# A linear-attention and feed-forward kernel: its written list of steps made anew, and the last block's rows stored in two halves

## The chip, the cores and the metric

The kernel runs on one core of a Trainium2 chip. A core has TensorE (PE in the profile; its weight loads are shown apart as PEld), VectorE (DVE), ScalarE (ACT), GpSimd (POOL) and SyncE (SP). SP only issues DMA transfers, on its own queue (q1 in the profile); GpSimd issues others on a second one (q0). The metric is the device time of one execution, in microseconds.

## The reference

The first part is a gated linear attention over 4 batches, 8 heads, 768 positions and a head width of 48. The second is a feed-forward layer over the 3072 rows that it gives.

```python
f = 1.0 / (1.0 + np.exp(-f_logit))                       # all inputs (4, 8, 768, 48)
for t in range(S):
    state = f[:, :, t, :, None] * state + np.einsum('bhd,bhe->bhde', k[:, :, t], v[:, :, t])
    y[:, :, t] = np.einsum('bhd,bhde->bhe', q[:, :, t], state)
x = y.transpose(0, 2, 1, 3).reshape(3072, 384)
h = x @ w_in                                             # (3072, 2048)
sp = np.maximum(h, 0.0) + np.log1p(np.exp(-np.abs(h)))
out = (h * erf(sp)) @ w_out                              # (3072, 384)
```

## The kernel before

**Tiles.** The positions are cut into 24 chunks of 128 rows, g = 0 to 23, six to a batch. Two chunks make a block of 256 tokens for the feed-forward part, so there are 12 blocks, 0 to 11. The 2048 hidden columns of a block are 4 groups of 512.

**A chunk, step by step.** f, q, k, v load the logits and the three inputs by SyncE (L263, L269, L276); w loads v a second time into the state tile `sv`, by GpSimd (L290). cl, ex, ln turn logits to log decays (VectorE L420, ScalarE L424, L428; for chunks from 4 on, two chunks at a time), d sums them on TensorE (L448, L456), e takes the exponentials (ScalarE L465), qd and kd multiply q and k by them (VectorE L479, L486). tx or tq, tk transpose on TensorE (L510, L501), aq and ak copy the transposes to SBUF (L524, and `kT` in the helper at L137). ds forms the products for the state (L576), sc the scores (L588), m masks the scores (VectorE L613), st adds to the running state (L550 to L553). td and tt send the decay totals out to DRAM and back by SyncE (L468, L473). sp copies the state into `sv`: on ScalarE or VectorE where the step names an engine, and else by a DMA of SyncE (L559, 22 of them). y forms the rows of x (L639) from qA and sv.

**A block, step by step.** h or hf, ht is x times w_in (L681 in plain fp32, L700 in three parts), c copies a hidden group out of PSUM (`h` at L137), ae, ax, aw, ah, at, au, am form the activation out of an exponential, three tanh and VectorE products (ScalarE L173, L176, L731; VectorE L181, L735), o or oa, ot is the product with w_out (L767), ro copies the rows out (`rows` at L137), so stores them (SyncE L805). Blocks 0 to 2 use plain fp32 in the first product, blocks 0 to 3 in the second; the later ones use weights split into parts, which are made in the first 200 us (r steps L328 to L353, kci, kMi, kDi and kco, kMo, kDo L359 to L367). The parts of w_out that do not fit are kept in DRAM and fetched for each block by GpSimd, 96 fetches of 384 KB (nc, no, L393).

**Buffers.** Fifteen SBUF slots of 128 x 1024 floats and four pairs of PSUM banks are shared by everything. A step names its slots after "@", and waits until the last user of that slot is done.

**Order.** Nothing schedules this work: `run_steps` walks one list of some 1,860 words, `STEPS`, and issues each step as it comes. A word is the step's name, its numbers, an engine letter (v VectorE, a ScalarE) and its slots: `ak0v@2` is the copy of the transposed k of chunk 0 by VectorE into slot 2. Each engine, and each DMA queue, works in the order in which its instructions come in this list. `z` steps (L438) are matmuls of a constant into a bank that nobody reads; they only keep TensorE busy. ScalarE reads its functions from tables: a step that needs another table than the last one loads it (L404, L176, L731, 1283 ns each in the trace).

Of the kernel before, what the change touches and what calls it, by code (L numbers as in the profile page):

```python
# [44 lines left out]
FP32 = mybir.dt.float32  # L45
# [36 lines left out]
def kernel(  # L82
# [229 lines left out]

    def round_step(i, step):
# [10 lines left out]
        words = raw.rearrange("p (a n w) -> p a n w", a=m, w=2)  # L324
        low, high = words[:, :, :, 0], words[:, :, :, 1]
# [476 lines left out]

    def store(blk):
        r = blk * TB
        nc.sync.dma_start(  # L805
            out=out[r : r + TB, :].rearrange("(t p) c -> p t c", p=P), in_=rows_of.pop(blk)
        )
# [20 lines left out]
    def pads(_):  # L828
# [12 lines left out]
        r1_4 h0_0@1 e2 r2_2 k3 r1_5 r3_0 qd2 p6 ln3 r2_3 to2@0 v3 kd2 v2_0_1a d3@2 r2_4 v2_1_1a
        v2_1_0a r1_6 tk2@3 e3 tq2 r2_5 h0_1 aq2@0 qd3 r2_6 p4 r5_0 ak2v@2 f7@1 v2_0_0a ta2 kd3
        ds2 c0_0a r3_1 sc2 st4 tk3@3 aw0_0@2 m2_1_1 to3@1 m2_0_1 f4@3 r3_2 tq3 ta3 m2_0_0 ak3v@4
        aq3@5 ds3 m2_1_0 st5 q4 sp4a sc3 v5 r3_3 sp5a y2_0@0 m3_0_0 r6_0 y2_1 p7 m3_1_0 h0_2@3
        m3_1_1 r4_0 r6_1 f5 ae0_0@0 st6 r6_2 sp6a r4_1 w4 x2a m3_0_1 y3_1@2 r4_2 q5 y3_0 r3_4 f6
        x3a r5_1 ax0_0@5 r3_5 h1_0@2 w5 st7 r3_6 r7_0 k5 v4 cl4 h0_3 r7_1 ex4 r4_3 r5_2 k4 r4_4
        r5_3 ln4 h1_1 c0_1a r4_5 r5_4 ae0_1@4 r4_6 d4@3 r5_5 h0_4@1 e4 p8 r7_2 kd4 qd4 c1_0a@6
        k6 r5_6 q6 tx4@3 r6_3 p9 h0_5 aq4@7 ak4v@8 r6_4 r7_3 r8_0 r6_5 to4@3 r7_4 d5@2 r6_6
        c0_2a ds4 f9@3 sc4 r7_5 h1_3@1 ta4 e5 m4_1_1 m4_0_1 sp7a kd5 v6 r7_6 k7 r9_0 to5@2 p10
        qd5 m4_1_0 tx5@0 r9_1 f8 h1_2 m4_0_0 ak5v@8 st8 aq5@9 r9_2 st9 q7 ds5 c1_1a@10 ta5 sc5  # L850
        p11 r9_3 h0_6@3 sp8a m5_1_1 r9_4 sp9a v7 st10 r10_0 r9_5 sp10a h0_7 m5_0_0 m5_0_1 r10_1
        m5_1_0 r9_6 y4_0@2 r10_2 c0_3a p13 y5_1@1 at0_0 y5_0 r11_0 y4_1 w7 r10_3 h1_5@3 x5a
# [397 lines left out]
```

## Time and profile before

| | us |
|---|---|
| median of 3 runs | 581.14 |
| the runs | 579.44, 581.14, 584.6 |
| the profiled execution | 582.41 |
| its span | 580.7 |

The profiled execution took 1.27 us more than the median, and 1.71 us of it lie outside the span. A row of the grouped views gives the line, the engine, the operation, out<-in, the count, then the busy time with the mean of one in ns, then the idle time of the engine just before these instructions, and what ended it. A row of the timeline gives the start, how long it took, the engine and the line; in brackets is what the engine waited for. An fp32 matmul leaves two records in the trace.

### The profile page before, as it was taken

To read this page: it belongs to the slowest core of one execution; us is meant where nothing else is said; L and a number is where in the kernel's file an instruction comes from. 1 tells how busy PE (TensorE), PEld (TensorE's weight loads), DVE (VectorE), ACT (ScalarE), POOL (GpSimd) and SP (SyncE) were. 2 spreads that over 40 slices of the span, in tenths; PEclk is the share of its full clock that TensorE was granted. 3 is DMA by queue.
4 is the path that set the end of the run, shared out by engine and by line. 5 is a ranking of instruction groups with operands and counts; after the bars stand their busy time and mean duration, and the time that the engine had idled before them with its cause. 6 is when DMAs were issued, how large, how long until landed. Compare 5 with 4: busy or idle time off the path is not lost.

```text
span 580.7 us, 14922 instructions
## 1 busy us (share of the span) xinstructions
PE 557.6 (96%) x6217; PEld 469.6 (81%) x6217; DVE 468.1 (81%) x663; ACT 428.0 (74%) x523; POOL 107.8 (19%) x191
## 2 busy tenths in 40 slices
PE   8889999999999999999899999989999999999995
PEld 8778888756678567788779979969889979899983
DVE  6889899999996794897489688689888878674980
ACT  4788469789999985788859868777838637837870
POOL 1003022000030012033014123131214216111220
PEclk9998999999999999999899999999999999999998
DMA  9987684300621346589249749655684788543581
GB/s 210 250 212 162 164 228 126 109 0 31 109 56 55 55 88 214 165 208 230 57 99 227 175 105 259 151 130 120 186 191 137 182 203 215 139 104 98 158 224 61
DMA packets 155698, 85.59 MB, mean 147 GB/s; under 512 B 132228, under 2 KB 135300, under 8 KB 155624
## 3 DMA queue, kind: packets, MB, share of 16 engines
q1 hardware_dynamic: 139112, 42.68, 32.3%
q0 software_dynamic: 16512, 41.89, 26.2%
q8 instruction: 51, 0.84, 0.6%
q14 instruction: 23, 0.19, 0.1%
HBM read 73.41 MB, written 9.51 MB: 143 GB/s over the span
## 4 chain that ended last, share of the span: by engine, by line
PE 60%; DVE 17%; ACT 13%; DMA 4%; issue 3%; SPq 1%; POOL 0%; ACTq 0%; DVEq 0%; POOLq 0%
PE pair L767 24%; PE pair L700 21%; PE pair L681 4%; DVE e L181 3%; PE pair L639 3%; DVE qA L613 2%; ACT x L176 2%; PE pair L438 2%; ACT qA L524 2%; PE pair L588 2%; DMA sv<-state 2%; ACT L404 2%; DVE raw_y L348 2%; PE pair L576 1%; PE pair L510 1%
## 5 line engine op out<-in xcount | busy, mean ns | idle before, releaser
L181 DVE SCALAR_TENSOR_TENSOR e<-x,e 128x1024 f32<-128x1024 f32 x96 | 117.0, 1220 | 20.7 <-ACT x L176 10.3
L176 ACT ACTIVATE x<-h,serf_bias 128x1024 f32<-128x1024 f32 x88 | 100.0, 1146 | 20.0 <-DVE h L137 8.2
L767 PE MATMUL pair<-plain_o,h 128*128 128x384 f32 x320 | 110.6, 492 | 0.0
L393 POOL DMA_DIRECT2D piece<-form_dram x96 | 53.5, 558 | 254.1 <-PE pair L767 139.3
L290 POOL DMA_DIRECT2D sv<-in_v_dram x84 | 52.8, 638 | 200.1 <-PE pair L639 174.1
L767 PEld LDWEIGHTS pair<-plain_o,h 128*128 128x128 f32 x320 | 58.5, 190 | 36.6 <-issue 0.8
L767 PE MATMUL pair<-piece,g 128*128 128x384 f32 x384 | 81.1, 345 | 0.8 <-DVE g L755 0.4
L700 PE MATMUL pair<-xT,form_x 128*128 128x256 f32 x432 | 77.9, 288 | 2.7 <-ACT h L137 2.3
L700 PE MATMUL pair<-xT,form_i 128*128 128x256 f32 x432 | 74.7, 281 | 0.0
L767 PEld LDWEIGHTS pair<-piece,g 128*128 128x128 f32 x384 | 65.7, 189 | 4.0 <-ACT xT L658 0.7
L700 PEld LDWEIGHTS pair<-xT,form_x 128*128 128x128 f32 x432 | 62.6, 189 | 7.2 <-ACT h L137 2.7
L681 PE MATMUL pair<-xT,plain_i 128*128 128x256 f32 x288 | 66.7, 389 | 0.6 <-ACT xT L137 0.6
L681 PEld LDWEIGHTS pair<-xT,plain_i 128*128 128x128 f32 x288 | 55.0, 194 | 9.6 <-ACT xT L137 0.8
L700 PE MATMUL pair<-xT,form_y 128*128 128x256 f32 x432 | 62.3, 282 | 0.0
L735 DVE TENSOR_TENSOR h<-h,e 128x1024 f32<-128x1024 f32 x44 | 53.5, 1219 | 10.6 <-ACT e L731 10.5
L700 PEld LDWEIGHTS pair<-xT,form_i 128*128 128x128 f32 x432 | 61.4, 189 | 0.0
L731 ACT ACTIVATE e<-e 128x1024 f32<-128x1024 f32 x48 | 50.7, 1056 | 13.6 <-DVE e L181 13.2
L700 PEld LDWEIGHTS pair<-xT,form_y 128*128 128x128 f32 x432 | 56.6, 188 | 0.8
L173 ACT ACTIVATE e<-h 128x1024 f32<-128x1024 f32 x44 | 46.3, 1052 | 6.8 <-PE pair L588 2.8
L137 ACT COPY h<-pair 128x1024 f32<-128x1024 f32 x33 | 33.3, 1008 | 15.8 <-PE pair L700 10.1
L613 DVE TENSOR_TENSOR qA<-pair,tri 64x256 f32<-64x256 f32 x96 | 40.4, 421 | 5.3 <-PE pair L588 2.5
L524 ACT COPY qA<-pair 64x512 f32<-64x512 f32 x48 | 27.8, 578 | 17.3 <-DVE kT L137 6.2
(105 smaller groups left out, 792.7 us busy)
## 6 DMA issues: line engine op xcount, KB each, us to landing
piece<-form_dram POOLq DMA_DIRECT2D x96, 384.0 KB, 4.0
raw_y<-in_moe_w_out_dram SPq DMA_DIRECT2D x8, 768.0 KB
vt<-in_v_dram SPq DMA_DIRECT2D x24, 192.0 KB
qn<-in_q_dram SPq DMA_DIRECT2D x24, 192.0 KB
kn<-in_k_dram SPq DMA_DIRECT2D x24, 192.0 KB
form_dram<-piece SPq DMA_DIRECT2D x12, 384.0 KB
out_dram<-rows SPq DMA_DIRECT2D x12, 384.0 KB
sv<-in_v_dram POOLq DMA_DIRECT2D x84, 48.0 KB, 3.3
```

The lines of the kernel that those rows point to most:

```text
L173: nc.scalar.activation(out=dst[:], in_=h, func=AF.Exp)
L176: nc.scalar.activation(out=dst[:], in_=h, func=AF.Tanh, bias=serf_bias[:, i : i + 1], scale=SERF_KAB[i][0])
L181: nc.vector.scalar_tensor_tensor(out=e[:], in0=x[:], scalar=SERF_KAB[i][2], in1=e[:], op0=ALU.add, op1=ALU.mult)
L290: nc.gpsimd.dma_start(out=svs[g % NSV][half(1 - r), r, c, :, PAD : PAD + D], in_=v[b, r::2, t0 : t0 + C, :].rearrange("a t d -> t a d"),)
L393: nc.gpsimd.dma_start(out=streams[i, blk, u], in_=form_dram[i, u])
L524: nc.scalar.copy(out=qAs[g][half(r), r].rearrange("p a (c t) -> p a c t", c=2), in_=ps[half(r)])
L613: nc.vector.tensor_tensor(out=to, in0=sc[half(c), r], in1=tri1[half(c)].unsqueeze(1).broadcast_to((C, HP, C)), op=ALU.mult,)
L681: nc.tensor.matmul(hts[blk, gi][:, 2 * i + j, :], lhsT=w[:, kt, j * P : (j + 1) * P], rhs=xTs[blk][:, 0, kt, :], start=(kt == 0), stop=(kt ...
L700: nc.tensor.matmul(hts[blk, gi][:, 2 * i + j, :], lhsT=w[:, kt, j * P : (j + 1) * P], rhs=x[:, kt, :], start=(blk, p) not in begun, stop=True,
L731: nc.scalar.activation(out=e[:], in_=e[:], func=AF.Tanh, scale=SERF_C)
L735: nc.vector.tensor_tensor(out=h, in0=h, in1=es.pop((blk, gi))[:], op=ALU.mult)
L767: nc.tensor.matmul(ots[blk][:, tt, 0:d_model], lhsT=lhs, rhs=rhs, start=("o", blk, tt) not in begun, stop=True, skip_group_check=True,)
```

## The change

The list `STEPS` is written anew from first to last, by a planner that is not part of the file, which counted GpSimd's transfers ahead of SyncE's and took durations from a trace. What is computed, and with which instructions, is the same but for four things:

- `z` matmuls: 48 before (29, 2, 2, 2, 7, 6), now 21 (10, 4, 1, 5, 1).
- copies change engine: ten `kT` copies go from VectorE to ScalarE; of the `h` copies fourteen go from ScalarE to VectorE and eight the other way; three `rows` copies and two state copies go to VectorE, one `rows` copy to ScalarE; of the small copies of v two go each way.
- the rows of the last block are copied and stored in two halves, the first by VectorE and the second by ScalarE, in place of one copy on ScalarE and one store.
- the places of the table loads follow from the order of the activations; there are 32 of them before and 24 now.

`ADDED` is an empty tuple, so that the branches on it never run. Lines of the changed file are shifted by 2 to 14 (the first product in plain fp32, L681, is L686; the second, L767, is L772).

```diff
+    ADDED = ()
...
-                out=low.bitcast(FP32), in0=low, scalar=2.0**-52, in1=high.bitcast(FP32),
+                out=sums if i in ADDED else low.bitcast(FP32), in0=low, scalar=2.0**-52, in1=high.bitcast(FP32),
...
+        elif i in ADDED:
+            nc.gpsimd.dma_start(out=dst, in_=sums, accum_op=ALU.add)
...
+    def copy_half(blk, tt, engine, n=None):
+        if blk not in rows_of:
+            rows_of[blk] = by_half(slot(n, "rows"))
+        copy_by(engine, rows_of[blk][:, tt, :], ots[blk][:, tt, 0:d_model])
+
+    def store_half(blk, tt):
+        r = blk * TB + tt * P
+        nc.sync.dma_start(out=out[r : r + P, :], in_=rows_of[blk][:, tt, :])
...
-        p0 f0@0 zb0@0 f1 v0 in0 q0 r0_0 k0 r0_1 cl0 q1 r0_2 ex0 cl1 r0_3 k1 ln0 ex1 z29 d0@1
...
-        am11_3 ot11_4 ot11_5 o11_3_0 o11_3_1 ro11a@13 so11
...
+        o11_3_0 o11_3_1 rh11_0v@0 sh11_0 rh11_1a sh11_1
...
+            "so": store, "rh": copy_half, "sh": store_half, "xa": x_part_a, "xb": x_part_b, "xt": x_part_t,
```

At four places the new order is shown as the engines see it. The numbers behind a name tell buffers of one kind apart.

**SyncE at the start**, the first loads before and after: `raw_x` is a piece of the weights, `lt` the logits, `vt`, `qn`, `kn` are v, q and k.

```order
L310 DMA raw_x_117<-in_moe_w_in_dram 128x3x512
L263 DMA lt<-in_f_logit_dram 128x8x48 x2
L276 DMA vt_84<-in_v_dram 128x8x48
L276 DMA qn_88<-in_q_dram 128x8x48
L276 DMA kn_90<-in_k_dram 128x8x48
L276 DMA qn_89<-in_q_dram 128x8x48
```

```order
L263 DMA lt<-in_f_logit_dram 128x8x48 x2
L276 DMA kn_90<-in_k_dram 128x8x48
L310 DMA raw_x_121<-in_moe_w_in_dram 128x3x512
L276 DMA vt_84<-in_v_dram 128x8x48
L276 DMA qn_88<-in_q_dram 128x8x48
L276 DMA kn_91<-in_k_dram 128x8x48
```

The two logit loads and a k now stand ahead of the first piece of weights.

**TensorE from the rows of chunks 4 and 5** (L639, now L644) **to the log sums of chunk 7** (L456, now L461); `xT` is the transposed x, `h_x` and `h` are finished hidden groups.

```order
L639 MATMUL pair_1028<-qA,sv_86 32x64 x16
L681 MATMUL pair_1107<-xT,plain_i_444 128x256 x12
L681 MATMUL pair_1143<-xT,plain_i_116 128x256 x12
L681 MATMUL pair_1175<-xT,plain_i_462 128x256 x6
L681 MATMUL pair_1191<-xT,plain_i_462 128x256 x6
L681 MATMUL pair_1175<-xT,plain_i_462 128x256 x6
L681 MATMUL pair_1191<-xT,plain_i_462 128x256 x6
L681 MATMUL pair_1229<-xT,plain_i_286 128x256 x12
L767 MATMUL pair_1256<-plain_o_800,h_x_533 128x384 x8
```

```order
L644 MATMUL pair_1061<-qA,sv_86 32x64 x32
L644 MATMUL pair_1097<-qA,sv_87 32x64 x32
L772 MATMUL pair_1133<-plain_o_772,h_x_655 128x384 x8
L686 MATMUL pair_1170<-xT,plain_i_120 128x256 x12
L686 MATMUL pair_1197<-xT,plain_i_348 128x256 x12
L772 MATMUL pair_1133<-plain_o_798,h_x_758 128x384 x4
L686 MATMUL pair_1235<-xT,plain_i_376 128x256 x12
```

The second product starts right behind the rows now and alternates with the first one, where five h steps stood between them before. Up to the log sums of chunk 7 TensorE has one h step, one o step and 27 `z` matmuls of difference: 23 h, 11 o and 48 z before, 24, 12 and 21 now.

**SyncE around the logits of chunks 14 and 15** (L269, four transfers each): `Tall<-total_dram` and `total_dram<-dp` are the totals, `sv<-state` the state copies.

```order
L473 DMA Tall<-total_dram 128x8x1
L276 DMA qn_89<-in_q_dram 128x8x48
L276 DMA vt_84<-in_v_dram 128x8x48
L276 DMA vt_85<-in_v_dram 128x8x48
L468 DMA total_dram<-dp_95 2x512
L269 DMA lt<-in_f_logit_dram 64x4x48 x4
L276 DMA kn_90<-in_k_dram 128x8x48
L269 DMA lt<-in_f_logit_dram 64x4x48 x4
L473 DMA Tall<-total_dram 128x8x1
L468 DMA total_dram<-dp_96 2x512
```

```order
L478 DMA Tall<-total_dram 128x8x1
L276 DMA qn_89<-in_q_dram 128x8x48
L276 DMA vt_84<-in_v_dram 128x8x48
L276 DMA kn_90<-in_k_dram 128x8x48
L473 DMA total_dram<-dp_95 2x512
L276 DMA vt_85<-in_v_dram 128x8x48
L269 DMA lt<-in_f_logit_dram 64x4x48 x4
L473 DMA total_dram<-dp_96 2x512
L269 DMA lt<-in_f_logit_dram 64x4x48 x4
L276 DMA qn_88<-in_q_dram 128x8x48
```

The queue's own order hardly differs. In the list the step that first needs these logits, `cl14`, stands some 25 us of TensorE's work behind the second of the loads now, and stood some 7 us behind it.

**ScalarE and SyncE at the end.** Before, the last copy is one of both halves, with one store (the second of the two stores in the last row):

```order
L137 COPY rows<-pair_6460 128x768
```

```order
L805 DMA out_dram<-rows 128x2x384 x2
```

Now ScalarE copies half of it (VectorE has a row of the same form), and SyncE stores two halves:

```order
L137 COPY rows<-pair_6424 128x384
```

```order
L819 DMA out_dram<-rows 128x2x384
L815 DMA out_dram<-rows 128x384 x2
```

The first half is copied and stored while TensorE works on the second.

More of the change, by code (lines that the diff above doesn't have):

```diff
@@ L324, in round_step @@
         words = raw.rearrange("p (a n w) -> p a n w", a=m, w=2)
+        sums = raw[:, 0:PIECE].bitcast(FP32).rearrange("p (a n) -> p a n", a=m)
         low, high = words[:, :, :, 0], words[:, :, :, 1]
@@ L841 @@
[L841 to L852, printed above, removed]
@@ L967 @@
[L967 to L972 removed]
+        f1@0 f0 k0 p0 zb0@0 in0 v0 cl1 q0 ex1 cl0 ex0 k1 ln0 z10 d0@1 e0 q1 kd0 r0_0 z4 to0@1 v1
@@ new lines @@
+        aw3_3@7 sp18v y8_0 v11 m9_1_1 o3_2_1 w10 m9_1_0 m9_0_1 st19 xa8 m9_0_0 ax3_3@0 xb8
+        y9_1@3 nc4_0@9 kMo0 y9_0 xt8 o3_1_0 sMo0 xa9 kDo0 ae3_3@8 xb9 sp19v xt9 hf4_0@3 at3_3
+        w11 kDo1 ht4_0 au3_3 o3_2_0 kco2@12@13 no4_0@5 kco3@0@10 sCo2 ah3_3 kMo2 hf4_1 kMo3 sMo2
+        ht4_1 kDo2 hf4_3@1 c4_0a@6 sMo3 kDo3 sCo3 hf4_2 ax4_0@12 am3_3 ae4_0@13 ht4_3 ht4_2
+        kco5@8@7 at4_0 o3_3_0 kco4@10@14 sCo5 kMo5 aw4_0@12 kMo4 sCo4 c4_1a@0 au4_0 sMo4 hf4_4@3
+        sMo5 kDo4 ae4_1@12 ht4_4 kDo5 ah4_0 o3_3_1 ax4_1@8 am4_0 aw4_1@10 at4_1 hf4_5
@@ new lines @@
+        au5_0 no5_0@5 aw5_1@12 hf5_6@2 ak12v@7 ah5_0 qd13 sc12@3 cl18 no5_1@9 ax5_1@10 ds12
+        am5_0 tx13@0 v14 ae5_1@7 ht5_6 q15 m12_1_0 m12_0_1 aq13@11 hf5_7 at5_1 st24 ak13a@10
+        ht5_7 m12_1_1 st25 sc13@0 sp24 m12_0_0 ds13 m13_1_0 ex18 o4_3_0 au5_1 sp25 m13_1_1 v15
+        m13_0_0 ln18 m13_0_1 y12_0@3 ka5_0@12@10 st26 y12_1 o4_3_1 ah5_1 kb5_0 sp26 st27 aw5_2@2
+        oa5_0@0 kt5_0 oa5_1 ro4a@13 sp27 o5_0_0_1 xa12 w14 am5_1 y13_1@1 ax5_2@1 so4 y13_0
+        o5_0_1_1 xb12 ka5_1@7@12 c5_3v@11 nc5_3@14 ot5_0 xa13 ae5_2@10 w15 ot5_1 xb13 xt12
@@ new lines @@
+        at10_1 sp46 aw10_1@5 kb10_0 oa10_0@1 oa10_1 m23_1_0 nc10_2@4 hf10_5 ro9v@8 nc10_3@9 ck0
+        so9 au10_1 ht10_4 ht10_5 ah10_1 o10_0_0_1 m23_1_1 kt10_0 c10_2a@5 y22_1@0 y23_1@2 am10_1
+        ae10_2@13 y23_0 y22_0 xa23 o10_0_1_1 xa22 xb23 ax10_2@8 ot10_0 xt23 xb22 ot10_1
+        ka10_1@6@11 at10_2 no10_2@14 hf11_0@0 no10_3@2 xt22 kb10_1 oa10_2 hf11_1 kt10_1 ht11_1
+        ht11_0 hf11_3@2 c11_0v@4 nc10_4@8 ht11_3 ae11_0@7 hf11_5@0 ax11_0@3 aw11_0@1 hf11_2
+        at11_0 ht11_2 ht11_5 c11_1v@3 hf11_4 aw10_2@10 au11_0 oa10_3 aw11_1@1 ht11_4 au10_2
@@ new lines @@
+        nc10_5@6 o10_1_1_1 ah11_0 hf10_6@2 ah10_2 am11_0 c11_2a@10 ht10_6 o10_1_0_1 ka11_0@7@9
+        ot10_2 ae11_1@11 kb11_0 ot10_3 no10_4@14 ax11_1@0 hf10_7 am10_2 at11_1 ht10_7
+        ka10_2@13@2 no10_5@12 hf11_7@0 kb10_2 c10_3a@0 oa10_4 kt10_2 oa10_5 ax10_3@8 o10_2_0_1
+        kt11_0 nc11_0@6 ae10_3@13 o10_2_1_1 au11_1 ot10_4 nc11_1@2 ht11_7 no11_0@14 at10_3
+        ah11_1 ot10_5 aw10_3@1 hf11_6 no11_1@5 aw11_2@12 au10_3 oa11_0@2 ht11_6 nc11_2@6
+        ax11_2@1 oa11_1 c11_3v@8 o11_0_1_1 ah10_3 nc11_3@2 am11_1 o11_0_0_1 ot11_0 am10_3
@@ L986, in run_steps @@
             "ka": part_a, "kb": part_b, "kt": part_t, "o": project, "ro": copy_rows,
-            "so": store, "xa": x_part_a, "xb": x_part_b, "xt": x_part_t,
+            "so": store, "rh": copy_half, "sh": store_half, "xa": x_part_a, "xb": x_part_b, "xt": x_part_t,
             "hf": hidden_parts("ab"), "ht": hidden_parts("t"),
```

236 lines of the change are left out of this document (112 added, 124 removed).

## The prediction

> **What bounds the kernel now.** I read the busy time by stage first. Columns: stretch in us, its length, busy us (and count) of PE, PEld, DVE, ACT and POOL, granted TensorE clock, DMA share, GB/s.
>
> ```profile
> 0.00:29.00 29.00, 24.71 (x390) 22.27 (x391) 22.45 (x53) 16.80 (x35) 3.08 (x13) 1.00 0.93 230
> 29.00:82.00 53.00, 49.60 (x611) 41.65 (x609) 48.46 (x90) 36.08 (x58) 6.88 (x11) 0.97 0.81 193
> 82.00:141.00 59.00, 59.00 (x349) 43.47 (x348) 58.87 (x73) 50.66 (x53) 6.96 (x9) 1.00 0.24 74
> 141.00:212.00 71.00, 69.41 (x750) 49.32 (x750) 60.09 (x83) 68.91 (x84) 5.44 (x9) 1.00 0.35 71
> 212.00:574.00 362.00, 354.90 (x4121) 312.90 (x4119) 278.19 (x368) 254.79 (x295) 85.48 (x150) 1.00 0.65 163
> 574.00:580.70 6.70, 0.00 (x0) 0.00 (x0) 0.00 (x0) 0.77 (x1) 0.00 (x0) 0.70 0.17 62
> ```
>
> Up to 82 us PE idles 4.3 + 3.4 = 7.7 us. From 82 to 141 PE and DVE are both full. From 141 to 212 PE idles 1.6 and ACT 2.1. Then PE alone bounds the time, idle 7.1 of 362 us. Behind its last matmul stands a tail of 6.7. No other order can take more out of PE's idle time than 7.7 + 1.6 + 7.1 = 16.4 us, except where PE does work of no use, which the next view shows: PE's records at the start, one h step, one o step and the log sums of chunk 7, then the group of all `z` matmuls.
>
> ```profile
> 1.65 9.09 PE L438 MATMUL pair<-tri 128*128 128x128 f32 x58 [1.65 <-POOL tri L1012]
> 10.57 0.81 PE L448 MATMUL pair<-lt,tri 128*128 128x384 f32 x2
> 29.09 2.75 PE L681 MATMUL pair<-xT,plain_i 128*128 128x256 f32 x12
> 44.34 4.44 PE L681 MATMUL pair<-xT,plain_i 128*128 128x256 f32 x12
> 133.21 2.74 PE L767 MATMUL pair<-plain_o,h 128*128 128x384 f32 x8
> 141.43 0.88 PE L456 MATMUL pair<-lt,tri 64*64 64x192 f32 x16 [0.30 <-ACT rows L137]
> L438 PE MATMUL pair<-tri 128*128 128x128 f32 x96 | 14.3, 313 | 1.6 <-POOL tri L1012 1.6
> ```
>
> An h step is 12 records in 2.75 us, an o step 8 in 2.74. The `z` steps fill 14.3 us, all before 82, so PE's room there is 7.7 + 14.3 = 22 us. The second h row took 4.44: its clock fell to half for one stretch of 3.41 us, which is the 0.97 of that stage's row (half of 3.41 is 3% of 53). Such a stretch costs about 1.7 us of work.
>
> **Part 1: up to the log sums of chunk 7.** Before, the first logits wait behind a piece of weights:
>
> ```profile
> 0.83 0.44 SPq L310 DMA_DIRECT2D raw_x<-in_moe_w_in_dram  x1
> 1.32 1.10 SPq L263 DMA_DIRECT2D lt<-in_f_logit_dram  x2
> 5.89 0.90 ACT L328 ACTIVATE plain_i<-raw_x 128x768 f32<-128x768 f32 x1 [3.78 <-DMA raw_x<-in_moe_w_in_dram]
> 6.82 0.56 DVE L330 TENSOR_SCALAR plain_i<-plain_i 128x768 f32<-128x768 f32 x1 [2.43 <-ACT plain_i L328]
> 7.29 0.35 DVE L420 TENSOR_SCALAR lt<-lt 128x384 f32<-128x384 f32 x1
> ```
>
> The clamp starts at 7.29 behind the rounding of the weights. With the logits first it can start about when ACT starts on the weights now, 5.89: 1.4 us earlier, but the weights come later, and their rounding shares DVE.
>
> By the log sums of chunk 7 (141.43) the new order has done one h and one o step more, 2.75 + 2.74 = 5.5 us of PE's work. I take 5.2, since a few small products stand behind that mark now. It is paid from the `z` time: 27 fewer, 27 x 2 records x 14.3 / 96 = 8.0 us. DVE must deliver more ahead of the mark too, at these prices:
>
> ```profile
> L181 DVE SCALAR_TENSOR_TENSOR e<-x,e 128x1024 f32<-128x1024 f32 x96 | 117.0, 1220 | 20.7 <-ACT x L176 10.3
> L362 DVE SCALAR_TENSOR_TENSOR form_y<-plain_i,form_x 128x768 fp32r<-128x768 f32 x8 | 7.4, 949 | 0.1
> L367 DVE SCALAR_TENSOR_TENSOR form_i<-form_y,form_x 128x768 fp32r<-128x768 f32 x8 | 7.5, 952 | 0.0
> L137 DVE COPY kT<-pair 128x512 f32<-128x512 f32 x21 | 14.5, 690 | 6.7 <-ACT qA L524 5.6 <-ACT sv L137 0.6
> ```
>
> Counted along both lists: two more activation products (2 x 1.22), four more weight parts (4 x 0.95), four `kT` copies fewer that ScalarE takes (4 x 0.69), and one clearing of a state tile fewer, taken as the shortest of these, 0.6: 2.4 + 3.8 - 2.8 - 0.6 = 2.8, say 2.9 us more on DVE. If DVE binds, the gain is 5.2 - 2.9 = 2.3; if PE binds, 5.2. I take 3, near the lower, since DVE is busy 58.87 of 59. The lower bound is below nothing: with fewer `z` the clock may stay at half. Three such stretches take 3 x 1.7 = 5.1, so 2.3 - 5.1 = -2.8. **3 us (-2.8 to 5.2).**
>
> One rule speaks against this part. The Trainium skill, "TensorE: Matmul & The Clock Gate", Part 1, says that the clock is halved whenever TensorE was not busy enough in a window of 3413 ns; the stretches of 3.41 us agree. By it ten `z` matmuls instead of 29 leave PE idle ahead of the first log sums, and the start runs cold, and the sum would go by the second rival below; by the rows, where DVE and not PE is full, it stays as it is.
>
> **Part 2: 141 to 212.** ACT is busy 68.91 of 71 and loads tables:
>
> ```profile
> L404 ACT ACT_TABLE_LOAD x16 | 20.5, 1283 | 1.1 <-PEq L1234 0.8
> L731 ACT ACT_TABLE_LOAD x9 | 11.5, 1283 | 0.2
> L176 ACT ACT_TABLE_LOAD x7 | 9.0, 1283 | 1.8 <-PE pair L767 1.6
> ```
>
> 32 loads become 24; five of the eight lie in this stage, 5 x 1.28 = 6.4 us of ACT. But PE idles only 1.6 here. The saving is capped by that: **1 us (0 to 1.6).** What ACT gets back pays for its new `kT` copies.
>
> **Part 3: 212 to 574, PE alone.** Its largest waits, in total, count, longest, and the places where they stand:
>
> ```profile
> PE pair L700 <- ACT h L137: 2.3, 1, 2.3
> PE pair L639 <- DMA sv<-state: 1.4, 2, 1.1
> 266.83 3.35 SPq L269 DMA_DIRECT2D lt<-in_f_logit_dram  x4
> 276.36 0.56 DVE L420 TENSOR_SCALAR lt<-lt 128x768 f32<-128x768 f32 x1 [3.10 <-DMA kn<-in_k_dram]
> 279.20 0.64 PE L700 MATMUL pair<-xT,form_x 128*128 128x256 f32 x3 [2.26 <-ACT h L137]
> 279.66 0.82 PE L700 MATMUL pair<-xT,form_i 128*128 128x256 f32 x3
> 383.40 1.89 SPq L559 DMA_DIRECT2D sv<-state  x2
> 384.05 4.71 DMA sv<-state
> ```
>
> The wait of 2.3 begins with the logits of chunks 14 and 15: issued from 263.46 to 270.2, they land at 276.3, DVE's clamp waits, the products behind it on DVE are late, so the copy of `h`, so PE. Its idling halves the clock for one more stretch (0.82 for three matmuls), 1.7 us. The list now has those loads 25 us of PE's work ahead of the clamp (7 before). No other pair of load and clamp is nearer than 7.4 us now, and four were nearer than that before, so I expect nothing in its place: 2.3 + 1.7 = 4.0 back.
>
> The second is a state copy by SyncE, 4.71 us in flight with 3.8 us of PE's work ahead of its use; it cost 1.1 + 0.4 = 1.5. The new list gives that one 5.1 us. But two others stand tighter: chunk 19's with 1.7 and chunk 13's with 2.1. Before, one with 2.6 waited for nothing, and one with 3.8 waited 1.5, that is, needed 5.3. So the two cost between (2.6 - 1.7) + (2.6 - 2.1) = 1.4 and (5.3 - 1.7) + (5.3 - 2.1) = 6.8. I take 2.9, nearer the lower end, since two waits in 22 copies are all the trace shows. **4.0 + 1.5 - 2.9 = 2.6 us.** At the top is all idle time and the half clock, 7.1 + 1.7 = 8.8. At the bottom 5.5 - 6.8 = -1.3, and below it the third rival. Which engine makes the `h` and `kT` copies costs nothing here: DVE is busy 278 and ACT 255 of 362 us, each with 80 and more to spare.
>
> **Part 4: the end.** The last copy and store:
>
> ```profile
> L137 ACT COPY xT<-pair 128x384 f32<-128x384 f32 x6 | 2.8, 474 | 2.8 <-PE pair L639 2.7
> 573.97 0.80 ACT L137 COPY rows<-pair 128x768 f32<-128x768 f32 x1 [7.67 <-PE pair L767]
> 574.80 0.37 SPq L805 DMA_DIRECT2D out_dram<-rows  x1
> ```
>
> The first half's copy and store lie beside the last o step (2.7 us). Behind it stays half a copy, 0.47 in place of 0.80, so 0.3, and a store of half the size. Of the 580.70 - 574.80 = 5.9 us from its issue to the end I take 0.2 off, and 0.7 as the most, since most of it must be the same for any size. **0.5 us (0.3 to 1).**
>
> The halves' functions, the shifted lines and the branch on an empty tuple issue nothing else and cost nothing.
>
> **Sum.** 3 + 1 + 2.6 + 0.5 = 7.1. Against the profiled execution: 582.4 - 7.1 = 575.3. That execution lay 1.27 above the median of 581.14, so the forecast for a median is 574.0.
>
> **Rivals.**
> *Within 1%, chance 0.36.* PE has at most 16.4 us idle before and the new list makes the paths to it tighter: activation ends and their o step stand under 5 us of PE's work apart at 14 places, 7 before; the same holds for the parts and their products. If each of the seven new places waits 0.5 us, the 7.1 shrink to 3.6: about 577.5. If waits eat parts 1 and 3 whole, part 2 and 4 remain: 579.6. Against it: mask and rows stand further apart now (32 places under 5 us, 51 before).
>
> *A cold start, no faster, chance 0.05.* PE's work of use up to 82 us is 24.71 + 49.60 - 14.3 = 60 us, in 24 stretches of 3.41. If eight of them run at half clock, 8 x 1.7 = 13.6 us are lost: 587.6. Beside 22 us of room it decides only from about four stretches on (6.8, which is the gain). For it: the 44.34 row. Against it: DVE, not PE, sets the pace there.
>
> *GpSimd's fetches come late, slower, chance 0.11.* Parts of w_out are fetched in a crowded window and in a quiet one with these latencies:
>
> ```profile
> piece<-form_dram POOLq DMA_DIRECT2D x4, 384.0 KB, 7.0
> piece<-form_dram POOLq DMA_DIRECT2D x2, 384.0 KB, 3.5
> q1 hardware_dynamic: 3457, 0.98, 49.0%
> q0 software_dynamic: 499, 1.11, 44.2%
> ```
>
> The crowded one (346 to 356 us) has q1 at 49.0% and q0 at 44.2%: neither stands ahead of the other there. If the list counts on GpSimd's being first, fetches that it places late come late. From a slot's release to the use of what is fetched into it are under 6 us of PE's work at 12 places now (least 4.9), 5 before. A late one costs 7.0 - 4.9 = 2.1. All 12 would take 25 us; slower from four on (7.1 / 2.1), slower by 1% from seven on: 574 + 7 x 2.1 = 588.7. Against it: neither of PE's two largest waits before is for a fetch.
>
> The Trainium skill, "DMA: Bandwidth & Descriptors", "Queues, rings and completion order", says each DMA engine goes round its queues packet by packet; the shares of q1 and q0 agree, and speak for this rival.
>
> **How the numbers follow.** The forecast's own case, in which most of the four parts come, has 0.48 and spans 569 to 577. A difference under about 1%, 5.8 us, is what a measurement of this kernel can hardly tell from none: faster is below 575.3, slower above 587. The forecast's case puts 0.38 below 575.3 and 0.10 above. Of the first rival's 0.36, 0.05 falls below, since its 577.5 is only 2.2 from that bound, and 0.31 within. Of the last two's 0.16, 0.13 lies above 587. That makes faster 0.43, same 0.10 + 0.31 + 0.03 = 0.44, slower 0.13. The upper end goes to 586, into the last two rivals; the lower to 566, near the top of all bounds together (5.2 + 1.6 + 8.8 + 1 = 16.6, that is 564.5).
>
> **What would show it.** Part 1: the first log sums before 9.5 us, those of chunk 7 no later than 141.4 us with `z` records down to 42, and clock 1.00 from 12 to 82 us. Part 2: 24 table loads. Part 3: no PE wait by the logits of chunks 14 and 15, no half clock near 280, PE idle there under 5 us; waits for `sv<-state` at the rows of chunks 13 and 19. Part 4: under 6.5 us from the last matmul to the end. Wrong, if PE waits for `piece` or `g` by several us, or if log sums of chunk 7 come later than 144.

## The result and the profile after

| | before | changed |
|---|---|---|
| median, us | 582.87 (579.44 to 585.76) | 572.29 (570.49 to 572.92) |
| profiled execution, us | 582.41 | 572.92 |
| span, us | 580.7 | 570.8 |

The ratio is 0.9845 with a 95% interval from 0.9806 to 0.9884. That is 1.6% faster, or 9.0 us (6.8 to 11.3) of 582.87. The medians are of four runs each. A second set of runs on another occasion gave 0.9815 (0.9788 to 0.9843), a median of 570.69 and a profiled execution of 569.28. Both executions of the changed kernel are read below: "the first" with a span of 570.8, "the second" with 567.2.

The busy time by stage of the first one, in the columns shown before; the third stage ends at the log sums of chunk 7, the fifth at the last matmul:

```profile
0.00:29.00 29.00, 23.93 (x416) 20.08 (x416) 20.78 (x52) 19.88 (x43) 2.77 (x13) 0.94 0.90 221
29.00:82.00 53.00, 50.01 (x518) 42.12 (x511) 49.68 (x83) 36.49 (x53) 6.67 (x11) 0.97 0.74 180
82.00:145.26 63.26, 62.26 (x397) 44.14 (x396) 62.10 (x81) 54.51 (x62) 5.62 (x9) 1.00 0.28 83
145.26:212.00 66.74, 66.74 (x693) 47.49 (x696) 54.82 (x82) 49.72 (x65) 5.47 (x9) 1.00 0.39 82
212.00:564.30 352.30, 349.48 (x4169) 309.81 (x4164) 282.90 (x372) 251.86 (x293) 85.53 (x150) 1.00 0.65 166
564.30:570.80 6.50, 0.00 (x0) 0.00 (x0) 0.52 (x1) 0.48 (x1) 0.00 (x0) 0.83 0.19 67
```

In the third and fourth stage together PE is idle 1.0 us, where it was idle 1.6, and in the fifth 2.8 us, where it was idle 7.1. ACT has 17 us free in the fourth stage, where it had 2. These rows don't say when the 10 us were won, since the same stretch holds other work now. For that I worked out how far PE had come at each moment. Each of its records counts with the mean time to the next record, by its kind (line and tiles), in the trace of before; the `z` matmuls count nothing; the difference of these sums at the same moment is PE's lead over the kernel before, in us.

```
at us      40    90   140   210   260   290   340   360   400   560
first    -0.7   3.3   1.1   3.6   3.9   9.1   9.3   5.1   8.1  10.2
second    0.2   4.4   3.4   5.3   5.6  10.3  10.7   8.9  12.1  13.8
```

Some 3 to 4 us come in the first 90 us, and 1 to 2 of them are given back by 140. Two come between 140 and 210, five between 260 and 290, three between 360 and 400, and the rest in small pieces. Around 350 the new order loses, 4.2 us in the first execution and 1.8 in the second. The two executions of one kernel differ by 2.3 us at 140, by 1.4 at 340 and by 3.8 at 360. One burst of small matmuls more or less moves such a sum by up to 1 us, so smaller differences between two moments say little.

**The start.** From the timeline PE's first log sums and those of chunk 7, and from the groups the `z` matmuls:

```profile
6.45 0.91 PE L453 MATMUL pair<-lt,tri 128*128 128x384 f32 x2 [0.54 <-ACT lt L433]
145.26 0.88 PE L461 MATMUL pair<-lt,tri 64*64 64x192 f32 x16
```

```profile
L443 PE MATMUL pair<-tri 128*128 128x128 f32 x42 | 8.2, 362 | 1.6 <-POOL tri L1026 1.6
```

The first log sums come at 6.45 in place of 10.57. Those of chunk 7 come 3.8 us later than before (143.26 in the second execution, 1.8 later), with more work done ahead of them. The two stretches in which the clock fell, in the columns of the stages:

```profile
13.60:20.40 6.80, 5.67 (x96) 5.17 (x100) 6.08 (x14) 4.99 (x12) 0.00 (x0) 0.75 0.96 229
34.00:40.80 6.80, 6.25 (x117) 5.44 (x118) 4.66 (x10) 2.71 (x5) 0.61 (x1) 0.75 1.09 240
```

A mean of 0.75 over 6.8 us is one stretch of 3.41 us at half clock in each. The trace of before has one such stretch by 82 us, and both executions here have two. That is not a mark of the order: the edited kernels below have one or two in either order, and one of them more.

**ScalarE's table loads** are 24 now, by line:

```profile
L409 ACT ACT_TABLE_LOAD x12 | 15.4, 1283 | 1.0 <-PEq L1248 0.8
L176 ACT ACT_TABLE_LOAD x10 | 12.8, 1283 | 0.6 <-PE pair L772 0.5
L736 ACT ACT_TABLE_LOAD x2 | 2.6, 1283 | 0.0
```

**PE's waits from 212 us to its last matmul**, the first execution's whole list, and where the largest of them stands:

```profile
PE pair L772 <- issue: 1.5, 1, 1.5
PE pair L515 <- DVE qd L484: 0.5, 1, 0.5
PE pair L593 <- DVE state L557: 0.4, 1, 0.4
PE pair L772 <- ACT g L747: 0.2, 1, 0.2
```

```profile
352.87 0.34 PE L772 MATMUL pair<-piece,g 128*128 128x384 f32 x1 [1.51 <-issue]
```

The waits for the copy of `h` (2.3 us) and for the state copies (1.4) are gone, and none for a fetched piece has come. What is new is a stop for nothing that the profile shows ("issue"), between the third and the fourth of four like matmuls. The second execution has one of 1.1 us at the same place. What follows parts the two: half clock in the first execution (the first row) and full clock in the second (the other row), and so the lead falls by 4.2 us in one and by 1.8 in the other.

```profile
353.50:356.90 3.40, 3.40 (x18) 3.24 (x11) 3.31 (x7) 1.35 (x3) 1.11 (x3) 0.50 1.08 263
351.40:354.80 3.40, 3.40 (x29) 3.29 (x23) 3.34 (x7) 1.35 (x3) 1.64 (x3) 1.00 1.19 294
```

**The end:**

```profile
558.90 5.32 PE L772 MATMUL pair<-plain_o,h 128*128 128x384 f32 x16
564.26 0.56 DVE L137 COPY rows<-pair 128x384 f32<-128x384 f32 x1 [5.71 <-PE pair L772]
564.85 0.90 SPq L815 DMA_DIRECT2D out_dram<-rows  x2
564.90 0.48 ACT L137 COPY rows<-pair 128x384 f32<-128x384 f32 x1 [7.60 <-DVE rows L137]
```

Both copies stand behind all sixteen matmul records of the last two o steps, and the second waits for the first. So the sentence ahead, that the first half is copied and stored while TensorE works on the second, is not what the kernel does: the list has both copies behind both o steps.

### The profile page after: what moved, and what is told of

Read it like the earlier page. It is cut to its first block, busy times and chain, and to the rows that moved or that the text cites. A ratio compares the mean times of both kernels' runs of the same rounds, so it can differ in the third digit from the quotient of the medians.

```text
span 570.8 us, 14831 instructions
## 1 busy us (share of the span) xinstructions
PE 552.4 (97%) x6163; PEld 463.6 (81%) x6163; DVE 470.8 (82%) x666; ACT 412.9 (72%) x513; POOL 106.1 (19%) x191
## 4 chain that ended last, share of the span: by engine, by line
PE 73%; DVE 11%; issue 5%; DMA 4%; ACT 4%; POOL 0%; SPq 0%; DVEq 0%; POOLq 0%; ACTq 0%
PE pair L772 34%; PE pair L705 23%; PE pair L686 6%; PE pair L644 3%; DVE e L181 2%; PE pair L593 2%; PE pair L515 2%; PE pair L581 2%; PE pair L461 1%; DMA piece<-form_dram 1%; DMA raw_y<-in_moe_w_out_dram 1%; DMA raw_x<-in_moe_w_in_dram 1%; DVE qA L618 1%; DMA sv<-state 1%; ACT qA L529 1%
## 5 line engine op out<-in xcount | busy, mean ns | idle before, releaser
L772 PE MATMUL pair<-plain_o,h 128*128 128x384 f32 x320 | 110.8, 493 | 0.2 <-DVE h L740 0.2
L398 POOL DMA_DIRECT2D piece<-form_dram x96 | 52.3, 547 | 276.9 <-PE pair L772 177.5
L772 PEld LDWEIGHTS pair<-plain_o,h 128*128 128x128 f32 x320 | 58.6, 190 | 37.0 <-DVE h L740 1.4
L772 PE MATMUL pair<-piece,g 128*128 128x384 f32 x384 | 81.2, 349 | 1.7 <-issue 1.5
L772 PEld LDWEIGHTS pair<-piece,g 128*128 128x128 f32 x384 | 66.9, 191 | 4.1 <-issue 0.9
L686 PE MATMUL pair<-xT,plain_i 128*128 128x256 f32 x288 | 65.1, 382 | 1.0 <-DVE plain_i L358 1.0
L686 PEld LDWEIGHTS pair<-xT,plain_i 128*128 128x128 f32 x288 | 54.2, 190 | 10.1 <-ACT plain_i L331 1.1
L772 PE MATMUL pair<-form_o,g 128*128 128x384 f32 x192 | 39.7, 341 | 0.0
L137 ACT COPY h<-pair 128x1024 f32<-128x1024 f32 x27 | 27.2, 1008 | 13.0 <-PE pair L705 6.0
```

The lines of the kernel that those rows point to most:

```text
L137: (engine.copy if engine is nc.scalar else engine.tensor_copy)(out=out, in_=in_)
L398: nc.gpsimd.dma_start(out=streams[i, blk, u], in_=form_dram[i, u])
L686: nc.tensor.matmul(hts[blk, gi][:, 2 * i + j, :], lhsT=w[:, kt, j * P : (j + 1) * P], rhs=xTs[blk][:, 0, kt, :], start=(kt == 0), stop=(kt ...
L772: nc.tensor.matmul(ots[blk][:, tt, 0:d_model], lhsT=lhs, rhs=rhs, start=("o", blk, tt) not in begun, stop=True, skip_group_check=True,)
```

## The experiments

Each of these is timed beside the kernel before. In diffs of the list only the words around a move are shown.

**The clamp later, in the kernel before.**

```diff
-        hf5_1 cl14 am4_3 ex14 ht5_1
+        hf5_1 am4_3 ht5_1
...
-        o4_2_1_1 ln14
+        o4_2_1_1 cl14 ex14 ln14
```

> The kernel before with one thing moved: the clamp and the exponential of the logits of chunks 14 and 15 stand directly ahead of their logarithm, about 12 us of TensorE's work later, and so behind the landing of the logits. Theory: the stop at 276 us (2.3 us of PE waiting plus about 1.7 us of one half-clock stretch) goes and is not replaced: about 4 us less, ratio near 0.993, no half-clock stretch near 280. Rival: the wait only moves to the decays behind it, or to another product: ratio 0.998 to 1.002.

The ratio was 0.9954 (0.9923 to 0.9984): 2.7 us less (0.9 to 4.5). In its trace, which is of the fastest of its twelve executions, PE leads the kernel before by 4.7 us at 290, and nothing was lost behind. The stretch around the stop, the same two rows of the kernel before and then of this one:

```profile
276.00:279.40 3.40, 1.14 (x10) 0.94 (x9) 1.69 (x2) 2.09 (x3) 0.00 (x0) 1.00 0.46 59
279.40:282.80 3.40, 3.40 (x16) 3.13 (x15) 0.00 (x0) 3.14 (x3) 0.00 (x0) 0.54 0.02 5
```

```profile
276.00:279.40 3.40, 3.40 (x38) 3.08 (x37) 0.54 (x1) 3.39 (x4) 0.54 (x1) 1.00 0.42 53
279.40:282.80 3.40, 3.40 (x28) 3.40 (x28) 1.91 (x3) 3.14 (x5) 0.00 (x0) 1.00 0.74 174
```

PE was busy 1.14 of 3.4 us and then at 0.54 of its clock; now it is busy throughout at full clock, with 66 records in place of 26. The theory holds, and its 4 us lie inside the interval. The mean gain is smaller than the trace's, for the stop is not always that long: in the six other traces with the old list at that place it is 1.1 to 2.3 us.

**Fewer table loads, in the kernel before.**

```diff
-        ht3_2 ln8 cl12
+        ht3_2 cl12
...
-        st12 ex8
+        st12 ex8 ln8
...
-        au3_0 ex12 ah3_0
+        au3_0 ah3_0
...
-        kd9 ex10 v10
+        kd9 ex12 ex10 ln10 ln12 v10
...
-        am3_3 ln10 sc9@1
+        am3_3 sc9@1
...
-        sp16v ln12 sCo0
+        sp16v sCo0
```

> The kernel before with three logarithms and one exponential moved next to the exponential of chunks 8 and 10, so that six or seven of ScalarE's table loads (1.283 us each, about 8 us in all) between 141 and 212 us are not needed; nothing else moves. Theory, that ScalarE sets the pace between 141 and 212 although PE shows only 1.6 us idle there: PE is 2 to 2.5 us further on at 212 us, and the end comes as much earlier, ratio near 0.996. Rival, that PE sets the pace there (as the prediction had it, 0 to 1.6): under 1 us, and the saved ScalarE time turns up as idle time of ScalarE.

1.0042 (1.0014 to 1.0070): 2.4 us longer, which neither expected. The profiled execution is the slowest of its twelve. The stage, and rows at its end:

```profile
141.00:212.00 71.00, 68.03 (x686) 47.99 (x684) 59.44 (x82) 63.84 (x80) 5.48 (x9) 1.00 0.35 71
```

```profile
205.78 1.58 ACT L424 ACTIVATE lt<-lt 128x768 f32<-128x768 f32 x2
207.40 1.58 ACT L428 ACTIVATE lt<-lt 128x768 f32<-128x768 f32 x2
211.25 1.16 ACT L524 COPY qA<-pair 64x512 f32<-64x512 f32 x2
212.45 0.69 PE L588 MATMUL pair<-qA,kT 48*64 48x64 f32 x32 [1.90 <-ACT qA L524]
```

ACT is busy 5.1 us less, five loads fewer are left in the stage, and PE's lead is -0.3 at 210. So the rival holds as far as that: the saved time of ScalarE did not reach PE. Then the moves make a stop of their own. They bring one exponential and two logarithms ahead of the copies of `qA`, which start at 211.25 in place of 209.37; PE stops for 1.9 us, and the half clock behind it makes a lag of 3.6 at 220. So the loss up to there is the price of what was put ahead of the copies, and not of fewer loads.

**Copies ahead of activations, in the kernel before.**

```diff
-        tx6@1 ae2_1@10 td7 o1_3_1 ak6v@11 q8 aq6@9
+        tx6@1 ak6v@11 aq6@9 ae2_1@10 td7 o1_3_1 q8
...
-        tx7@0 kci6 v8 am2_0 h2_4 ax2_1@11 tt7 ak7v@4 aq7@0
+        tx7@0 ak7v@4 aq7@0 kci6 v8 am2_0 h2_4 ax2_1@11 tt7
...
-        tx8@3 k10 o3_0_1@0 ae3_3@4 q10 ak8v@11 aq8@12
+        tx8@3 ak8v@11 aq8@12 k10 o3_0_1@0 ae3_3@4 q10
```

> The kernel before with the copies of the transposed q and k (qA, kT) of chunks 6, 7 and 8 put ahead of the activation step that stood before them. Fewer table loads alone brought PE nothing up to 210 us, and the changed kernel has no waits for such copies between 145 and 212 us. Theory, that the gain of that stretch is these waits: they go (1.3 us in the trace of before, for L576 and L588), PE is 1 to 1.5 us further on at 180 us, ratio near 0.998. Rival: ScalarE, which stands still for the transposes, hands the time back: no lead at 212 us, ratio 1.000 or above.

1.0064 (1.0038 to 1.0089): 3.7 us longer. PE lags by 2.6 at 210, so the rival is right in sign and too mild. But the theory is not tested by this edit, for the waits did not go: in the trace L576 waits 0.25 and 1.21 us for the copies of `qA` of chunks 6 and 7, where it waited 0.45 and 0.34. The new stop, of a kind that neither named:

```profile
163.37 1.59 PE L639 MATMUL pair<-qA,sv 128*32 128x64 f32 x96 [1.90 <-ACT h L137]
```

ScalarE stands idle 1.03 and 1.86 us ahead of these two copies, and is late with the copy of a hidden group (162.30 in place of 159.93); PE waits for that in the middle of the rows of a chunk.

**The start alone, in the kernel before**, with 29 and with 10 `z` matmuls.

```diff
-        p0 f0@0 zb0@0 f1 v0 in0 q0 r0_0 k0 r0_1 cl0 q1 r0_2 ex0 cl1 r0_3 k1 ln0 ex1 z29 d0@1
+        f0@0 zb0@0 f1 k0 p0 v0 in0 q0 cl0 ex0 ln0 cl1 r0_0 q1 r0_1 r0_2 r0_3 k1 ex1 z29 d0@1
```

> The kernel before with the start alone reordered: both logit loads and one k ahead of the first piece of weights, and their clamp, exponential and logarithm ahead of the rounding; the 29 keep-busy matmuls stay. Theory, that the first log sums set the start: they cannot come before the 29 matmuls are done (1.65 + 9.09 = 10.7 us), so the gain is under 0.5 us. Rival, that the rounding on VectorE sets it: the time gets up to 1.4 us longer.

> As the run with the start reordered, but with 10 keep-busy matmuls in place of 29 ahead of the first log sums. Theory: the first log sums come near 6.5 us in place of 10.6, and PE is 1 to 1.5 us further on at 30 us; at the end 1 us less or so, as VectorE is full afterwards. Rival, the cold start: one or more half-clock stretches of 3.41 us between 10 and 40 us, 1.7 us each at most, which take the gain back, so that the time is that of the run with 29 or longer.

With 29: 1.0045 (1.0007 to 1.0082), 2.6 us longer, PE 1.1 behind at 60. No gain, as the theory had it, and the rival's loss on top. With 10: 1.0063 (1.0031 to 1.0096), 3.7 us longer. Its first two log sums and the clock behind them:

```profile
5.96 0.81 PE L448 MATMUL pair<-lt,tri 128*128 128x384 f32 x2
10.64 1.65 PE L448 MATMUL pair<-lt,tri 128*128 128x384 f32 x2 [3.43 <-ACT lt L428]
```

```profile
10.20:20.40 10.20, 9.07 (x118) 8.05 (x122) 8.02 (x18) 4.48 (x11) 0.00 (x0) 0.50 1.00 246
```

The first log sums did come early, at 5.96. Then PE stood still for 3.43 us and ran at half clock for the next 10 us, and lagged by 3.6 us at 35. That is the cold start. The changed kernel has ten `z` matmuls there too, but other work between its first two log sums, and its clock falls for one stretch in the first 30 us.

**More `z` matmuls, in the changed kernel**: 4, 1, 5 and 1 become 6, 3, 12 and 4.

```diff
-        r0_0 z4 to0@1
+        r0_0 z6 to0@1
...
-        q2 z1 tq0
+        q2 z3 tq0
...
-        z5 sc1
+        z12 sc1
...
-        z1 y0_0
+        z4 y0_0
```

> The changed kernel with 14 more keep-busy matmuls in the gaps of its first 23 us (4, 1, 5 and 1 become 6, 3, 12 and 4). Theory, that its two half-clock stretches between 17 and 34 us cost it something: at least the first goes, and PE is 0.5 to 1.5 us further on at 50 us. Rival, that VectorE sets the pace there and a slow PE is hidden: no lead, 0.5 us or so longer where a z stands in the way; in both cases under what the times can tell, so the traces decide.

PE leads the second execution by less than 1 us at 30, lags by 0.5 at 50 and is level at 260. Its two half-clock stretches lie between 35 and 43 us now, where the second execution has them at 19.5 and 29.7: the added matmuls moved them and took none away, so this run does not show what they cost. The other traces with this start don't show a price either: PE's lead at 140 is 3.1 to 4.4 us in the three with one stretch and 1.1 to 3.4 in the three with two. The ratio is 0.9881 (0.9837 to 0.9926), above both of the changed kernel's and overlapping with them. In the profiled execution, the slowest of six, what was lost lies at 261 and 351, two stops for "issue" of 1.8 us each with half clock behind, far from the edit.

**The `kT` copies of chunks 0 to 3**, by ScalarE in the kernel before, and back on VectorE in the changed one (`ak0a` to `ak3a` become `ak0v` to `ak3v`). For chunk 0, the three others alike:

```diff
-        ds0 ak0v@2 v0_0_0a
+        ds0 ak0a@2 v0_0_0a
```

> The kernel before with one part of the change: the kT copies of chunks 0 to 3 on ScalarE in place of VectorE. Theory, that VectorE sets the pace up to 141 us in the kernel before too: 2.8 us less on it brings the log sums of chunk 7 about 2.5 us earlier than 141.4, and the end as much, ratio near 0.996. Rival, that it only pays beside the new order's start (the copies back on VectorE cost the changed kernel 3.3 us): within 0.7 us here, ratio 0.999 to 1.001, or longer, as ScalarE is late with its first exponentials.

> The changed kernel with the kT copies of chunks 0 to 3 back on VectorE (four of 0.69 us, 2.8 us of VectorE's time in the first 80 us). Theory, that VectorE sets the pace up to the log sums of chunk 7: those come 2 to 3 us later than the 145.3 us of the changed kernel, and the end as much later. Rival, that ScalarE or the DMAs set it at the start: under 0.7 us.

The changed kernel itself was run in the same set:

> The changed kernel itself, as the measure for the three others of this set: 572 us, ratio 0.984 to the kernel before.

It came out at 0.9815, 570.69 us. With the copies back on VectorE it is 0.9872 (0.9848 to 0.9897), 574.16 us: 3.5 us longer, and the log sums of chunk 7 come at 146.54 in place of 143.26. In the kernel before the same move gives 0.9988 (0.9961 to 1.0016), the log sums of chunk 7 0.8 us later. So the copies are worth 3 us beside the new start and nothing beside the old one: the theory holds for the changed kernel, the rival for the one before. A row of the changed kernel with the copies back shows what VectorE's time is for. The same products start at 19.94 and 19.36 in the two executions of the changed kernel, 2.0 and 2.6 us earlier:

```profile
21.97 0.29 PE L593 MATMUL pair<-qA,kT 48*64 48x64 f32 x4 [1.67 <-DVE state L557]
```

**More table loads, in the changed kernel.** A new step puts in a load of the exponential's table, after which the next tanh loads its own.

```diff
+        "tl": lambda _: (other_set(), use_exp_ln(), other_set()),
...
-        ah2_2
+        tl0 ah2_2
...
-        ax2_3@5
+        tl1 ax2_3@5
...
-        ah2_3
+        tl2 ah2_3
```

> The changed kernel with three pairs of table loads put in between about 165 and 190 us (six of 1.283 us, 7.7 us of ScalarE's time in a stage in which it is now busy 49.7 of 66.7 us). Theory, that in the changed kernel ScalarE has 17 us to spare there and no longer sets the pace: under 1.5 us longer. Rival, that the loads lie on the path of the activations whatever the sum: 4 us or more.

0.9928 (0.9901 to 0.9955), 577.03 us: 6.3 us longer than the changed kernel. The rival is right. The profiled execution is the fastest of its six, and 4.2 of the 6.3 us are in its trace. Where they come from:

```profile
175.40 1.28 ACT L176 ACT_TABLE_LOAD   x1
176.69 1.15 ACT L176 ACTIVATE x<-h,serf_bias 128x1024 f32<-128x1024 f32 x1
177.75 0.99 ACT L137 COPY h<-pair 128x1024 f32<-128x1024 f32 x1
178.79 1.01 PE L705 MATMUL pair<-xT,form_x 128*128 128x256 f32 x3 [3.35 <-ACT h L137]
```

One copy of a hidden group comes late behind the loads, PE waits 3.35 us for the banks, and half clock follows: PE lags the second execution by 4.8 us at 190, and by 4.2 at the end. ScalarE's 17 free us in this stage did not help: from 165 to 179 us it was busy without a gap, so the free time lies elsewhere.

**The first half's copy between the last two steps, in the changed kernel.**

```diff
-        o11_3_0 o11_3_1 rh11_0v@0 sh11_0 rh11_1a sh11_1
+        o11_3_0 rh11_0v@0 sh11_0 o11_3_1 rh11_1a sh11_1
```

> The changed kernel with the first half's copy and store put between the last two steps of the second product instead of behind both. In the trace of the changed kernel the first half's copy starts only after the last matmul (564.26 us) and ScalarE's copy waits for it until 564.90. Theory: the first half goes beside the last matmuls, the second half's copy starts 0.6 us earlier, and the end comes 0.5 to 1 us earlier. Rival: what is left of the store's own time is the same for any size and order, under 0.3 us.

0.9824 (0.9794 to 0.9855), 571.06 us: no difference from 0.9815 that the times can show, though their interval of 3.5 us would hide the 0.5 to 1 us of the theory. So its rows decide:

```profile
557.32 0.56 DVE L137 COPY rows<-pair 128x384 f32<-128x384 f32 x1 [3.14 <-PE pair L772]
557.90 3.81 SPq L815 DMA_DIRECT2D out_dram<-rows  x2
557.93 2.85 PE L772 MATMUL pair<-plain_o,h 128*128 128x384 f32 x8 [0.65 <-DVE rows L137]
560.86 0.48 ACT L137 COPY rows<-pair 128x384 f32<-128x384 f32 x1 [7.94 <-DVEq L1232]
```

The copy does start early, but the last o step writes the same pair of banks and waits 0.65 us for it. From the last matmul to the end are 6.1 us in place of 6.6, so the wait takes what the earlier copy wins.

**The logits late again, in the changed kernel.**

```diff
-        kd11 f15@3 kt4_0
+        kd11 kt4_0
...
-        ka4_1@7@14 f14 au4_2
+        ka4_1@7@14 au4_2
...
-        ms12 v13 xa10
+        ms12 v13 f14@3 k14 f15 xa10
...
-        tt13 ht5_3 k14 ax5_0@0
+        tt13 ht5_3 ax5_0@0
```

In this kernel the k of chunk 14 is loaded over that of chunk 12 before chunk 12 uses it, so chunk 12 and what follows from it are computed from other numbers, with the same instructions.

> The changed kernel with the loads of the logits of chunks 14 and 15 put back to 7.4 us of TensorE's work ahead of their clamp, with a load of k between them as before (25 us in the changed kernel). Theory, that this distance is what took the stop at 276 us away: a stop of 1.5 to 2.5 us comes back there, with a half-clock stretch behind it in most executions, 2 to 4 us longer than the changed kernel: ratio 0.986 to 0.990. Rival, that it was the work around the clamp and not the distance: no wait by the clamp, ratio 0.980 to 0.985.

0.9850 (0.9807 to 0.9894), 571.46 us, within what the changed kernel itself gave on two occasions. The clamp:

```profile
268.44 0.56 DVE L425 TENSOR_SCALAR lt<-lt 128x768 f32<-128x768 f32 x1 [2.02 <-DMA lt<-in_f_logit_dram]
```

VectorE waits 2.02 us for the logits again (in the row of before, the wait is put down to a load of k issued among them), and yet PE's lead over the second execution is 0.3 at 280: PE was not waiting for what stood behind the clamp. The rival is wrong that the clamp does not wait, and right about PE: the distance is not what took the stop away. That it was the work behind the clamp agrees with this and with the clamp moved alone, but no run changes that work by itself.

## Why the prediction was right, and where its terms were off

The time, 572.29, lies 1.7 below the forecast of 574.0 and inside its range. The gain is 9.0 us beside the forecast 7.1, or 8.85 from the 581.14 that the forecast started from. By its bound of 1% it is faster, to which it gave 0.43 against 0.44 for no change. Term by term it was less right than the sum: in the two traces the four parts come to 10.4 and 14.0 us in place of 7.1. It is in part luck that the time lies so near. The 2.9 us set aside for two state copies never fell due, and a stop at 350 us, which nothing in the prediction foresaw, took 4.2 and 1.8 us.

*Part 1, 3 us (-2.8 to 5.2).* PE's lead at 140 is 1.1 in the first execution and 3.4 in the second, so the size was about right. That VectorE sets the pace is borne out in the changed kernel: 2.8 us of copies put back on it cost 3.5 us. It fails as a statement on the kernel before, where the same 2.8 us taken off brought nothing. "Log sums of chunk 7 no later than 141.4 us" was wrong, and the text's own limit of 144 was passed in the first execution. That sign did not follow from the sum: with 2.9 us more work on a VectorE that sets the pace they come 2.9 us later, at 144.3. They came 3.8 and 1.8 later. VectorE's busy time up to them grew by 2.4 and 2.2 us, a little less than counted, and in the first execution it also stood idle 1.5 us longer; PE's work of use ahead of them grew by 5.3 us, as counted. So that they are late says nothing while PE leads. The clock of 1.00 did not come either. The second rival, a cold start, was right for the old order (3.6 us behind at 35) and not for the new one, where work fills PE between its first log sums. Its "24 stretches" are those of all 82 us; 60 us of work fill 17.6 of them, which changes nothing in the sum.

*Part 2, 1 us (0 to 1.6).* Probably mis-sized: 1.9 to 2.5 between 140 and 210, above its bound, which was PE's idle time of 1.6 us; the excess is within what one burst of matmuls moves these sums. The kernel before has these waits of PE in that stage (us in all, times, longest), and the changed kernel has none in either execution:

```profile
PE pair L576 <- ACT qA L524: 0.8, 2, 0.4
PE pair L588 <- ACT qA L524: 0.5, 2, 0.3
PE pair L456 <- ACT rows L137: 0.3, 1, 0.3
```

They go, and perhaps a little more that no wait shows. The 24 table loads came as counted. But they are not shown to be the cause: five loads fewer in the kernel before brought nothing by 210. Nor are the three waits, for the edit that put copies ahead did not take them away. What loads cost depends on what stands behind them (3.35 us of PE's time for one late copy). Which of the many moves in this stage wins the 2 us stays open.

*Part 3, 2.6 us (down to -1.3, up to 8.8).* Mis-sized: 6.6 us in the first execution (10.2 less 3.6) and 8.5 in the second. Of its three pieces, the 4.0 for the stop at the logits of chunks 14 and 15 came, 5 us of lead between 260 and 290, and the clamp moved alone gives 2.7 by the times. Its reason was half right: with the loads as late as before the clamp waits again in the new order, but PE does not. The 1.5 of the state copy came too, with what follows it, 3 us between 360 and 400; in the seven traces of the old list at that place the wait appears in four, 1.1 to 1.9 us long. The step that failed is the third, "I take 2.9" for two tighter state copies. Neither waited. Rows of the first execution at chunk 19, which was given 1.7 us of PE's work:

```profile
424.60 1.24 SPq L564 DMA_DIRECT2D sv<-state  x2
427.43 1.99 PE L644 MATMUL pair<-qA,sv 128*32 128x64 f32 x128
```

```profile
sv<-state SPq DMA_DIRECT2D x4, 36.0 KB, 3.4
```

The copy is issued from 424.60 on, and the matmuls that use it are the last quarter of the 128, from about 428.9: 4.3 us later, where the list gave 1.7. The median landing in this stretch (second fence) is 3.4 us, not the 4.71 of the crowded one. PE's work between two words of the list is not the time between two events: SyncE does not wait until PE gets to the word.

*Part 4, 0.5 us (0.3 to 1).* 0.2 by the spans, under its lower end: 580.70 - 573.93 = 6.8 from the last matmul to the end before, 570.80 - 564.22 = 6.6 now, and 6.6 in the second execution. The "under 6.5 us" that was to show it did not come. That the first half lies "beside the last o step" was a misreading of the list, and putting it there wins nothing, because the last o step then waits for the copy.

*The other rivals.* PE waited for a fetch by GpSimd once each in three of the edited kernels, 0.9 to 1.2 us, and in neither execution of the changed one: the 12 tight places are not a price of 2.1 each. The first rival, new waits of small size, was wrong in kind: the small waits got fewer. Its place is taken by the stop at 350, which no case had: 1.0 to 2.6 us in six of the seven traces of the new order. In the first execution's stretch from 348 to 352 us the two data queues have 62.0% and 48.8%, and an instruction queue has a transfer of 16 KB (0.02 MB) among them, rows of the queues in that stretch:

```profile
q1 hardware_dynamic: 2536, 0.29, 62.0%
q0 software_dynamic: 241, 0.54, 48.8%
q8 instruction: 1, 0.02, 2.0%
```

No edit was made for it, but the traces show that PE waits there for its own instructions. The queue q8 makes 50 such transfers for the 12,484 records of PE and its weight loads, about one for each 250. Counted over these records, the stops without a cause in the profile end at record 7873 in five traces of the new order, at 7874 and 5570 in the one with more `z` matmuls, and at 10946 in the old order with the copies ahead. These places lie whole multiples of 256 apart, to within one, and each of the eight stops ends 1.3 to 1.6 us after a transfer of q8 has landed. The 28 matmul records of the added `z` steps left the stop at 350 at its place in the count and moved it to another matmul (L593 in place of L772). With each transfer paired in this way to the 256 records that it brings, no trace of the fourteen has PE at the first of them sooner than 1.27 us after the landing; the median is some 8 us. In the first execution this transfer starts 3.2 us after PE has begun the 256 records before, and PE is through those in 4.3 us. Why the transfer starts that late is open; that the two data queues keep it back was not tried.

## What to carry to other kernels

Single moves taken out of a rewritten order don't add up to it: of six edits to the old order one paid, one made no difference and four cost 2.4 to 3.7 us, while of five small edits to the new order two cost 3.5 and 6.3 and none paid. So look for the stop that a late engine passes on to PE (a clamp at the head of VectorE's queue, a copy of a hidden group behind a table load), and change what stands behind the late instruction rather than only the transfer ahead of it. Judge by how far PE has come at the same moment, not by busy shares, and take two traces of a kernel before explaining a difference of 3 us.

## What was not expected of the hardware

PE can stop between two matmuls that have all they need, because its next instructions have not come. It happened where many small matmuls follow each other (256 records in 4.3 us ahead of the stop in the first execution), and always a whole multiple of 256 apart in the count of PE's records, to within one; it took 1.0 to 2.6 us.

A stop of some 2 us can cost twice its length, because the clock falls behind it: without the stop of 2.3 us at 276 PE was 4.7 us further on at 290. How long a stop may be can be read from the fourteen traces, from 60 us to the last matmuls. All five stops of 2.08 us and more have a half-clock stretch behind them, none of the seventeen from 0.88 to 1.45 us has one, and of the seven from 1.51 to 1.90 us five have.
